# Fewer changes of TensorE tiling: row-tiled groups shifted by one tile across layer borders in a six-layer cross network

## The chip, the cores and the metric

The kernel runs on one core of a Trainium2 chip. The metric is the device time of one execution in microseconds (us), smaller is better. The times of before are three runs on the chip; the profile is one further execution taken by the hardware profiler. All times below are us from the start of the profiled span unless they are said to be run times. TensorE is called PE, its weight loads PEld, VectorE DVE, ScalarE ACT, GpSimd POOL, SyncE SP.

## The reference

```python
B, F, D, L = 4096, 26, 16, 6
Din = min(F * D, 1024)            # 416
# x0: [4096, 416], ws: [6, 416, 416], bs: [6, 416], all bf16
def reference(x0, ws, bs):
    x = x0
    for l in range(ws.shape[0]):
        x = x0 * (x @ ws[l] + bs[l]) + x
    return x
```

Six layers, each a 416 x 416 matrix product for 4096 rows, a bias, a product with x0 and a sum with the layer's input.

## The kernel before

**Layout.** For the first five layers the activations lie transposed: features on partitions, rows of the batch along the free dimension. The 416 features are three blocks of 128 (`XM`, index k or m) and a remainder of 32. The batch of 4096 is two halves s = 0, 1 of 2048 columns, each of four column groups g of 512. The remainder of the four groups of one half is stacked on the 128 partitions of `XR` (32 partitions for each g). `XM[0]`, `XR[0]` hold x0; `XM[1]`, `XM[2]` and `XR[1]`, `XR[2]` take turns as a layer's input and output.

**Three tilings of PE.** A 128-feature output block is made of two kinds of matmuls. The three main blocks contract 128 partitions: in the first layer as whole-array matmuls (`full` in `first_layer`, L240), in layers 1 to 4 *column-tiled* (`mm_full`, L205): four matmuls with 32 output columns each at positions (0, 0), (0, 32), (0, 64), (0, 96), which run side by side. The remainder contracts 32 partitions and is *row-tiled* (`mm_row`, L211; in the first layer `row`, L247): four matmuls at positions (0, 0), (32, 0), (64, 0), (96, 0), one for each column group. The product for the remainder's own 32 output features (`mm_rem`, L217 and L222) is column-tiled. A *tile* below is one output block m of one half s: four PSUM banks, as two pairs (`new_pts`, two calls of `two_banks`, which hands out the four pairs of banks in a fixed order).

**Order of work.** The order is written out by hand, each engine runs its instructions in program order. `first_layer(0)` and `first_layer(1)` do the first layer; `rem_first` the remainder of both halves at its end. In each of layers 1 to 4 the six tiles (0,0), (0,1), (0,2), (1,0), (1,1), (1,2), as (s, m), are worked in three couples ta, tb: `mm_full` of ta, then one row-tiled group that closes ta and opens tb (`mm_row` twice), then `mm_full` of tb. So each layer has three row-tiled groups. After the first couple come the remainders of both halves (`rem_pair`).

**Behind a tile.** `finish` calls `ew_main` for each pair of banks: ACT copies PSUM to a bf16 buffer `t` with the bias added (L169; six such buffers), which frees the banks; DVE multiplies by x0 (L179) and adds the layer's input (L180). The first layer folds the sum into the bias, so that DVE only multiplies (L177); `split_first` shares one pair between ACT (L186) and DVE (L187). `ew_rem` does the same for the remainder (L193, L198, L199).

**Last layer.** Here the roles are swapped: 128 rows of the batch are the output's partitions and 416 features its columns, so the result lies in row order. There are eight row tiles q (`quads`), each of four column groups g. Each needs 12 whole-array matmuls (`mm_q_full`, L357), and row-tiled ones for the remainder (L366) and the bias (L371) in `mm_q_rows`. Row tiles 0 to 5 go in couples with one row-tiled group each, 6 and 7 have one each: five groups. ACT casts (L383, single ones L396), DVE multiplies by `X0rows` (L384, L397) and adds `XLrows` (L385, L400), SP stores. `XLrows` is layer 4's output turned into row order: DMA transposes on SP for the main blocks (`xl_dmat`, L229), and for the remainder a DMA transpose into `scrR` (L299) and a copy by POOL (L300).

**Loads.** All go through SP's queue in the order of the code, but for the first layer's weights, the biases and the layer-0 rows of `WR`, which ACT issues at the start. `WR` holds the 32 remainder rows of the weights four times, once for each row position: for layer 0 one load and three copies by DVE (L113), for layers 1 to 5 four loads on SP. `WD` (POOL, L133) holds their block-diagonal form for the remainder's own product. `load_x0t` (L77) loads and transposes 512 columns of x0.

Of the kernel before, what the change touches and what calls it, by code (L numbers as in the profile page):

```python
# [10 lines left out]
ALU = mybir.AluOpType  # L11
BF16 = mybir.dt.bfloat16
# [4 lines left out]
def kernel(  # L17
# [7 lines left out]
    nc = tc.nc  # L25
    B, D = x0.shape
    L = ws.shape[0]
    P = 128
# [68 lines left out]
    load_x0t(0, 0)  # L97
    load_wm(nc.scalar, 0)
    nc.scalar.dma_start(bsb[0:L, :], bs[:, :])
    load_wr(nc.scalar, 0, 0, 1)  # L100
    nc.scalar.activation(dz[:, 1:2], dz[:, 0:1], ACT.Identity, bias=dz[:, 0:1], scale=1.0)

    nc.vector.transpose(out=bT[:], in_=bsb[0:R, :].rearrange("p (c r) -> p c r", r=R))
# [7 lines left out]
        nc.gpsimd.tensor_copy(bsb[32 * g:32 * g + 32, :], bsb[0:R, :])  # L111
    for g in range(1, NG):
        nc.vector.tensor_copy(WR[32 * g:32 * g + 32, 0, :], WR[0:32, 0, :])  # L113
    load_x0t(0, 1)
    load_xrem(nc.sync, 0, 0, 64)
    load_x0t(0, 2)
# [5 lines left out]
    load_x0t(1, 3)  # L122
    load_wm(nc.sync, 1)
    for g in range(NG):
        load_wr(nc.sync, g, 1, L)
    for l in range(2, L):
        load_wm(nc.sync, l)
    for q in range(8):
# [12 lines left out]

    def two_banks():
        n = turn[0]
        i = first_order[n] if n < len(first_order) else (2, 1, 3, 0)[(n - len(first_order)) % 4]
        turn[0] += 1
        return PS[:, 2 * i:2 * i + 2, :]

# [77 lines left out]
    def new_pts():  # L225
        return [two_banks() for h in range(2)]
# [4 lines left out]

    def first_layer(s):
        cur, nxt = XM[0], XM[1]

        def full(pt, m, h, gl, first, last):
            c0 = col0(s, 2 * h + gl)
            for k in range(NK):
                nc.tensor.matmul(pt[:, gl, :], lhsT=WM[:, 0, k, 128 * m:128 * m + 128], rhs=cur[:, k, c0:c0 + CW],  # L240
                                 start=(first and k == 0), stop=(last and k == NK - 1), skip_group_check=True)

        def row(pt, m, h, swapped, first):
            for gl in range(2):
# [14 lines left out]
        if s == 0:  # L259
            closing = [split_first(s, 0, 0, pa[0], nxt)]  # L260
            closing.append(split_first(s, 2, 0, pa[2], nxt))
            t1 = ew_copy(0, 1, pa[1])
            for close in closing:
                close()
            x0_rem(0, 64, 128, (nc.scalar.copy, nc.vector.tensor_copy))
            nc.vector.tensor_tensor(out=nxt[:, 1, 0:2 * CW], in0=t1, in1=XM[0][:, 1, 0:2 * CW], op=ALU.mult)
        else:
            split_first(s, 0, 0, pa[0], nxt)()
            for m in (2, 1):
                ew_main(0, s, m, 0, pa[m], cur, nxt)  # L270
        pb += [two_banks() for m in range(1, NK)]
        for m, gl in ((0, 0), (1, 0), (2, 0), (0, 1), (1, 1), (2, 1)) if s == 0 else ((0, 0), (1, 0), (0, 1), (1, 1), (2, 0), (2, 1)):
            full(pb[m], m, 1, gl, s == 0 or m > 0, s == 1 and m == 0)
            if s == 1 and (m, gl) == (0, 1):
                ew_main(0, s, 0, 1, pb[0], cur, nxt)
        if s == 0:
            row(pb[0], 0, 1, 0, False)
            row(pb[1], 1, 1, 0, False)
            row(pb[2], 2, 1, 1, False)
            split_first(s, 0, 1, pb[0], nxt)()  # L280
            x0_rem(1, 0, 128, (nc.vector.tensor_copy,))
            for m in range(1, NK):
                ew_main(0, s, m, 1, pb[m], cur, nxt)
        else:
            row(pb[1], 1, 1, 0, False)
            row(pb[2], 2, 1, 1, False)
            rem_first(pb)

    x0_rem(0, 0, 64, (nc.scalar.copy, nc.vector.tensor_copy))
    load_xrem(nc.scalar, 0, 64, 128)  # L290
# [9 lines left out]
                nc.gpsimd.tensor_copy(XLrows[:, 16 * s:16 * s + 16, NK * P:D].rearrange("p (g i) r -> p i g r", g=NG),  # L300
                                      scrR[s][:].rearrange("p i (g r) -> p i g r", g=NG))

    def rem_first(pb):
        pr2 = two_banks()
        for s in range(NS):
            mm_rem(0, s, pr2[:, s, :], XM[0], XR[0])
        for s in range(NS):
            ew_rem(0, s, pr2[:, s, :], XR[0], XR[1])
            ew_main(0, 1, 1 + s, 1, pb[1 + s], XM[0], XM[1])

    first_layer(0)
    fill_wd(1, L)
    first_layer(1)
    cur, curR = XM[1], XR[1]
    for l in range(1, LL):
        nxt, nxtR = XM[1 + (l % 2)], XR[1 + (l % 2)]
        feeds_last = (l == LL - 1)
        tiles = [(s, m) for s in range(NS) for m in range(NK)]
        pts = {}

        def finish(t):
            s, m = t
            for h in range(2):
                ew_main(l, s, m, h, pts[t][h], cur, nxt)
            if feeds_last:
                xl_dmat(s, m, nxt)

        for n in range(0, len(tiles), 2):
            ta, tb = tiles[n], tiles[n + 1]
            pts[ta] = new_pts()  # L330
            for g in range(NG):
                mm_full(l, ta[0], ta[1], g, pts[ta], cur, True, False)
            mm_row(l, ta[0], ta[1], pts[ta], curR, False, True)
            pts[tb] = new_pts()
            mm_row(l, tb[0], tb[1], pts[tb], curR, True, False)
            finish(ta)
            for g in range(NG):
                mm_full(l, tb[0], tb[1], g, pts[tb], cur, False, True)
            finish(tb)
            if n == 0:  # L340
                rem_pair(l, cur, curR, nxtR, feeds_last)
        cur, curR = nxt, nxtR

    l = LL
    quads = [(s, i) for s in range(NS) for i in range(4)]
    NQ = len(quads)
    KD = NK * P

    def q_cols(q, g):
        s, i = quads[q]  # L350
# [3 lines left out]
    def mm_q_full(q, py, gs, first):  # L354
        for g in gs:
            for k in range(NK):
                nc.tensor.matmul(py[g // 2][:, g % 2, 0:D], lhsT=cur[:, k, q_cols(q, g)], rhs=WM[:, l, k, :],  # L357
                                 start=(first and k == 0), stop=((not first) and k == NK - 1), skip_group_check=True)


# [1 line left out]
    def mm_q_rows(qs, pys, begun):  # L362
        for q, py in zip(qs, pys):
            s, i = quads[q]
            for g in range(NG):
                nc.tensor.matmul(py[g // 2][:, g % 2, 0:D], lhsT=curR[32 * g:32 * g + 32, CW * s + 128 * i:CW * s + 128 * i + 128],  # L366
                                 rhs=WR[32 * g:32 * g + 32, l, :], start=not (q == begun and g < 2), stop=False,
                                 tile_position=(32 * g, 0), skip_group_check=True)
        for q, py in zip(qs, pys):
            for g in range(NG):  # L370
                nc.tensor.matmul(py[g // 2][:, g % 2, 0:D], lhsT=pick[1][32 * g:32 * g + 32, :],  # L371
                                 rhs=bsb[32 * g:32 * g + 32, :], start=False, stop=(q == begun and g < 2), tile_position=(32 * g, 0),
                                 skip_group_check=True)

    o4 = [big.tile([P, NG, D], BF16, name=f"o4_{q}") for q in range(3)]

    def ew_pair(q, h, py):
        s, i = quads[q]
        b0 = 16 * s + 8 * h + i
        t = tpool.tile([P, 2 * CW], BF16, name="t")  # L380
        tv = t[:, 0:2 * D].rearrange("p (a d) -> p a d", a=2)
        o = o4[q][:, 2 * h:2 * h + 2, :] if q < 3 else opool.tile([P, 2, D], BF16, name="o")[:]
        nc.scalar.copy(tv, py[h][:, :, 0:D])  # L383
        nc.vector.tensor_tensor(out=tv, in0=tv, in1=X0rows[:, b0:b0 + 5:4, :], op=ALU.mult)  # L384
        nc.vector.tensor_tensor(out=o, in0=tv, in1=XLrows[:, b0:b0 + 5:4, :], op=ALU.add)  # L385
        if q >= 3:
            nc.sync.dma_start(out_v[:, b0:b0 + 5:4, :], o)
        elif h == 1:
            nc.sync.dma_start(out_v[:, b0 - 8:b0 + 5:4, :], o4[q][:])

    def ew_single(q, g, py):
        s, i = quads[q]
        b = 16 * s + 4 * g + i
        t = tpool.tile([P, 2 * CW], BF16, name="t")
        o = opool.tile([P, 2, D], BF16, name="o")
        nc.scalar.copy(t[:, 0:D], py[g // 2][:, g % 2, 0:D])  # L396
        nc.vector.tensor_tensor(out=t[:, 0:D], in0=t[:, 0:D], in1=X0rows[:, b, :], op=ALU.mult)  # L397

        def close():
            nc.vector.tensor_tensor(out=o[:, 0, :], in0=t[:, 0:D], in1=XLrows[:, b, :], op=ALU.add)  # L400
            nc.sync.dma_start(out_v[:, b, :], o[:, 0, :])

        return close

    for q in range(0, NQ - 2, 2):
        py = [new_pts()]
        mm_q_full(q, py[0], (0, 1), True)
        py.append(new_pts())
        mm_q_rows((q, q + 1), py, q)
        ew_pair(q, 0, py[0])  # L410
        mm_q_full(q, py[0], (2, 3), False)
        ew_pair(q, 1, py[0])
        for h in range(2):
            mm_q_full(q + 1, py[1], (2 * h, 2 * h + 1), False)
            ew_pair(q + 1, h, py[1])
    pending = []
    for q in range(NQ - 2, NQ):
        py = new_pts()
        mm_q_rows((q,), (py,), None)
        for g in range(NG):  # L420
            mm_q_full(q, py, (g,), False)
            pending.append(ew_single(q, g, py))
            keep = 0 if (q, g) in ((NQ - 2, NG - 1), (NQ - 1, 0), (NQ - 1, NG - 1)) else 1
            while len(pending) > keep:
                pending.pop(0)()


# [28 lines left out]
```

## Time and profile before

| What | Value |
|---|---|
| Run times, median (lowest to highest) of 3 | 130.79 us (130.72 to 131.23) |
| Profiled execution: its own time | 130.19 us |
| Profiled execution: span on the page | 128.1 us |
| PE busy, matmuls | 122.7 us (96%), 1677 |
| DVE busy | 105.2 us (82%) |
| ACT busy | 83.5 us (65%) |
| POOL busy | 8.6 us (7%) |
| Granted PE clock | 1.0 |
| L205 column-tiled matmuls | 1152, 379 ns each, 65.2 us busy together |
| L357 last layer, whole array | 96, 340 ns each, 17.9 us busy |
| L169 ACT copy of a pair of banks | 56, 1115 ns each |
| L179, L180 DVE, 1024 columns | 48 each, 695 and 699 ns |

Busy time of matmuls that run side by side counts once, so 1152 matmuls of 379 ns make 65.2 us. The end of a matmul in the profile is modelled, and pipelined matmuls overlap; the pace of PE is read from one start to the next. Idle time of an engine costs only where another waits for it.

### The profile page before, as it was taken

Reading aid. Unit: us, or ns where it says so; the run is one execution under the profiler, and the core shown is the slowest. Engines: PE = TensorE matmul, PEld = TensorE weight load, DVE = VectorE, ACT = ScalarE, POOL = GpSimd, SP = SyncE. Lnnn points to the kernel's source line nnn. Section 1 sums busy time; section 2 is a strip of 40 time slices with the busy share of each in tenths; the row PEclk is TensorE's granted clock in tenths of the full one; section 3 lists DMA queues with packets and bytes.
Section 4 is the critical chain, followed back from the end, with each engine's and each line's share of the span. In section 5 each row is a group of like instructions: output and inputs, shape, how many; then the busy total and the mean of one; then the engine's idle time right before and its main releaser. Section 6 shows DMA issues by size and latency. Waiting matters only on the chain. (4 is left out here: it accounts for less than half of the span.)

```text
span 128.1 us, 3929 instructions
## 1 busy us (share of the span) xinstructions
PE 122.7 (96%) x1677; PEld 54.7 (43%) x1677; DVE 105.2 (82%) x192; ACT 83.5 (65%) x94; POOL 8.6 (7%) x29
## 2 busy tenths in 40 slices
PE   6999999999999999999999999999999999999960
PEld 3344344444444444444444544444444445445420
DVE  3347959357979898989898989898989999999991
ACT  2117559489666849666849666749666777567860
POOL 4282000120000000000000000000000300000000
PEclk9999999999999999999999999999999999999999
DMA  3999999999990000000000000000398899986663
GB/s 91 259 157 192 207 187 263 229 329 332 336 314 24 5 0 8 0 0 5 0 5 0 5 0 5 0 0 5 69 140 177 167 122 246 192 283 216 210 225 103
DMA packets 42029, 16.36 MB, mean 128 GB/s; under 512 B 30838, under 2 KB 42012, under 8 KB 42012
## 3 DMA queue, kind: packets, MB, share of 16 engines
q1 hardware_dynamic: 40512, 15.70, 55.0%
q10 hardware_dynamic: 1500, 0.42, 1.6%
q8 instruction: 13, 0.21, 0.7%
q14 instruction: 4, 0.03, 0.1%
HBM read 6.15 MB, written 3.41 MB: 75 GB/s over the span
## 5 line engine op out<-in xcount | busy, mean ns | idle before, releaser
L169 ACT ACTIVATE t<-PS,bM 128x1024 bf16<-128x1024 f32 x56 | 58.1, 1115 | 21.2 <-PE PS L211 21.2
L205 PE MATMUL PS<-XM,WM 128*32 128x512 bf16 x1152 | 65.2, 379 | 0.0
L205 PEld LDWEIGHTS <-WM 128*32 128x32 bf16 x1152 | 29.8, 97 | 33.7 <-issue 5.1
L179 DVE TENSOR_TENSOR t<-t,XM 128x1024 bf16<-128x1024 bf16 x48 | 33.4, 695 | 4.1 <-ACT t L169 4.1
L180 DVE TENSOR_TENSOR XM<-t,XM 128x1024 bf16<-128x1024 bf16 x48 | 33.5, 699 | 3.1
L357 PE MATMUL PS<-WM,XM 128*128 128x416 bf16 x96 | 17.9, 340 | 0.0
L240 PE MATMUL PS<-XM,WM 128*128 128x512 bf16 x72 | 16.5, 383 | 0.1
L383 ACT CAST t<-PS 128x832 bf16<-128x832 f32 x12 | 10.2, 852 | 5.0 <-PE PS L357 2.5
L357 PEld LDWEIGHTS <-XM 128*128 128x128 bf16 x96 | 8.9, 98 | 8.7 <-issue 2.1
L240 PEld LDWEIGHTS <-WM 128*128 128x128 bf16 x72 | 6.9, 99 | 9.4 <-issue 2.1
L222 PE MATMUL PS<-XM,WM 128*32 128x512 bf16 x120 | 8.2, 379 | 0.0
L193 ACT ACTIVATE t<-PS,bR 128x512 bf16<-128x512 f32 x10 | 6.8, 694 | 1.9 <-POOL WD L133 1.9
L385 DVE TENSOR_TENSOR o<-t,XLrows 128x832 bf16<-128x832 bf16 x12 | 7.1, 592 | 0.5
L211 PE MATMUL PS<-XR,WR 32*128 32x512 bf16 x96 | 7.3, 379 | 0.0
L384 DVE TENSOR_TENSOR t<-t,X0rows 128x832 bf16<-128x832 bf16 x12 | 7.0, 586 | 0.0
L300 POOL COPY XLrows<-scrR 128x512 bf16<-128x512 bf16 x2 | 1.4, 698 | 72.7 <-DMA scrR<-XR 72.7
L177 DVE TENSOR_TENSOR XM<-t,XM 128x1024 bf16<-128x1024 bf16 x7 | 4.7, 690 | 1.5 <-ACT t L169 1.4
L150 PE MATMUL PS<-warm 128*128 128x512 bf16 (+2 forms) x13 | 4.6, 536 | 1.0 <-DVE warm L87 1.0
L186 ACT ACTIVATE t<-PS,bM 128x512 bf16<-128x512 f32 x4 | 2.6, 685 | 3.8 <-PE PS L247 3.8
L162 ACT COPY XR<-xrt 64x256 bf16<-64x256 bf16 x2 | 1.2, 621 | 5.7 <-DVE xrt L161 5.7
L161 DVE STREAM_TRANSPOSE xrt<-xrem 64x256 bf16<-64x256 bf16 (+1 forms) x5 | 2.2, 477 | 3.2 <-DMA xrem<-in_x_dram 3.2
L396 ACT CAST t<-PS 128x416 bf16<-128x416 f32 x8 | 4.0, 506 | 1.0 <-PE PS L357 0.8
(44 smaller groups left out, 54.4 us busy)
## 6 DMA issues: line engine op xcount, KB each, us to landing
X0rows<-in_x_dram SPq DMA_DIRECT2D x8, 416.0 KB, 7.5
WM<-in_ws_dram SPq DMA_DIRECT2D x5, 312.0 KB, 6.7
out_dram<-o SPq DMA_DIRECT2D x3, 416.0 KB, 3.2
out_dram<-o SPq DMA_DIRECT2D x6, 208.0 KB, 2.5
out_dram<-o SPq DMA_DIRECT2D x8, 104.0 KB, 1.7
WR<-in_ws_dram SPq DMA_DIRECT2D x4, 130.0 KB, 5.7
WM<-in_ws_dram ACTq DMA_DIRECT2D x1, 312.0 KB, 3.4
XM<-in_x_dram SPq DMA_TRANSPOSE x8, 4.8
```

Of the source, the lines that this page charges most:

```text
L169: nc.scalar.activation(t[:], pt.rearrange("p a b -> p (a b)"), ACT.Identity, bias=bM[:, m, l:l + 1], scale=1.0)
L179: nc.vector.tensor_tensor(out=t, in0=t, in1=x0c, op=ALU.mult)
L180: nc.vector.tensor_tensor(out=nxt[:, m, c0:c0 + 2 * CW], in0=t, in1=cur[:, m, c0:c0 + 2 * CW], op=ALU.add)
L193: nc.scalar.activation(tr[:, 0:CW], pr, ACT.Identity, bias=bR[:, l:l + 1], scale=1.0)
L205: nc.tensor.matmul(pts[g // 2][32 * q:32 * q + 32, g % 2, :], lhsT=WM[:, l, k, 128 * m + 32 * q:128 * m + 32 * q + 32], rhs=cur[:, k, c0:c ...
L211: nc.tensor.matmul(pts[g // 2][:, g % 2, :], lhsT=WR[32 * g:32 * g + 32, l, 128 * m:128 * m + 128], rhs=curR[32 * g:32 * g + 32, CW * s:CW ...
L222: nc.tensor.matmul(pr[32 * g:32 * g + 32, :], lhsT=WM[:, l, k, NK * P:D], rhs=cur[:, k, c0:c0 + CW], start=False, stop=(k == NK - 1), tile ...
L240: nc.tensor.matmul(pt[:, gl, :], lhsT=WM[:, 0, k, 128 * m:128 * m + 128], rhs=cur[:, k, c0:c0 + CW], start=(first and k == 0), stop=(last ...
L357: nc.tensor.matmul(py[g // 2][:, g % 2, 0:D], lhsT=cur[:, k, q_cols(q, g)], rhs=WM[:, l, k, :], start=(first and k == 0), stop=((not first ...
L383: nc.scalar.copy(tv, py[h][:, :, 0:D])
L384: nc.vector.tensor_tensor(out=tv, in0=tv, in1=X0rows[:, b0:b0 + 5:4, :], op=ALU.mult)
L385: nc.vector.tensor_tensor(out=o, in0=tv, in1=XLrows[:, b0:b0 + 5:4, :], op=ALU.add)
```

## The change

- Layers 1 to 4: the couples that share a row-tiled group move on by one tile. A group now closes the second tile of a couple and opens the first of the next; the last group of a layer opens tile (0,0) of the next layer. Each layer's first tile is thus already open, with four PSUM banks held, when the layer begins. The remainder pair (`rem_pair`) stands after the third tile instead of after the second.
- First layer: the half s = 1 uses column-tiled matmuls instead of whole-array ones. The remainder of s = 0 stands inside it (`rem_first(0)`), that of s = 1 after the first tile of layer 1 (`rem_first(1)`). Its last row-tiled group also opens layer 1.
- Last layer: the last group of layer 4 also holds the rows and biases of row tile 0; tiles 1 and 2, 3 and 4, 5 and 6 share a group, 7 has its own: four groups. Within a group the biases of a tile follow its rows. The last half of row tile 5 is handled in single column groups as 6 and 7 are, and the order of the DVE steps of the last three tiles is written out as a list.
- Loads: the layer-1 rows of `WR` come with those of layer 0 on ACT's queue, and ACT makes their three copies. The fixed order of bank pairs changes from (2, 1, 3, 0) to (2, 1, 0, 3).

```diff
-    load_wr(nc.scalar, 0, 0, 1)
+    load_wr(nc.scalar, 0, 0, 2)
...
         nc.vector.tensor_copy(WR[32 * g:32 * g + 32, 0, :], WR[0:32, 0, :])
+        nc.scalar.copy(WR[32 * g:32 * g + 32, 1, :], WR[0:32, 1, :])
...
-        load_wr(nc.sync, g, 1, L)
+        load_wr(nc.sync, g, 2, L)
...
-        i = first_order[n] if n < len(first_order) else (2, 1, 3, 0)[(n - len(first_order)) % 4]
+        i = first_order[n] if n < len(first_order) else (2, 1, 0, 3)[(n - len(first_order)) % 4]
...
-                nc.tensor.matmul(pt[:, gl, :], lhsT=WM[:, 0, k, 128 * m:128 * m + 128], rhs=cur[:, k, c0:c0 + CW],
-                                 start=(first and k == 0), stop=(last and k == NK - 1), skip_group_check=True)
+                for q0, q1 in ((0, P),) if s == 0 else [(32 * q, 32 * q + 32) for q in range(4)]:
+                    nc.tensor.matmul(pt[q0:q1, gl, :], lhsT=WM[:, 0, k, 128 * m + q0:128 * m + q1], rhs=cur[:, k, c0:c0 + CW],
+                                     start=(first and k == 0), stop=(last and k == NK - 1),
+                                     tile_position=(0, q0) if s == 1 else None, skip_group_check=True)
...
+        full(pb[0], 0, 1, 0, False, False)
+        rem_first(0)
+        pb += [two_banks() for m in range(1, NK)]
+        full(pb[1], 1, 1, 0, True, False)
+        full(pb[0], 0, 1, 1, False, True)
+        ew_main(0, s, 0, 1, pb[0], cur, nxt)
+        full(pb[1], 1, 1, 1, True, False)
+        for gl in range(2):
+            full(pb[2], 2, 1, gl, True, False)
+        row(pb[1], 1, 1, 0, False)
+        row(pb[2], 2, 1, 1, False)
+        pt = new_pts()
+        mm_row(1, 0, 0, pt, XR[1], True, False)
+        for m in range(1, NK):
+            ew_main(0, s, m, 1, pb[m], cur, nxt)
+        return pt
...
         for n in range(0, len(tiles), 2):
             ta, tb = tiles[n], tiles[n + 1]
-            pts[ta] = new_pts()
             for g in range(NG):
-                mm_full(l, ta[0], ta[1], g, pts[ta], cur, True, False)
-            mm_row(l, ta[0], ta[1], pts[ta], curR, False, True)
+                mm_full(l, ta[0], ta[1], g, pts[ta], cur, False, True)
+            close(ta)
+            if n == 0 and l == 1:
+                rem_first(1)
+            if n == 2:
+                rem_pair(l, cur, curR, nxtR, feeds_last)
             pts[tb] = new_pts()
-            mm_row(l, tb[0], tb[1], pts[tb], curR, True, False)
-            finish(ta)
             for g in range(NG):
-                mm_full(l, tb[0], tb[1], g, pts[tb], cur, False, True)
-            finish(tb)
-            if n == 0:
-                rem_pair(l, cur, curR, nxtR, feeds_last)
...
+                mm_full(l, tb[0], tb[1], g, pts[tb], cur, True, False)
+            mm_row(l, tb[0], tb[1], pts[tb], curR, False, True)
+            opened = new_pts()
+            if n + 2 < len(tiles):
+                tc_ = tiles[n + 2]
+                mm_row(l, tc_[0], tc_[1], opened, curR, True, False)
+                pts[tc_] = opened
+            elif not feeds_last:
+                mm_row(l + 1, 0, 0, opened, nxtR, True, False)
+            else:
+                mm_q_rows((0,), (opened,), None)
+            close(tb)
...
+    order = [(0, 0), (0, 1), (1, 0), (2, 0), (1, 1), (3, 0), (4, 0), (2, 1), (5, 0), (3, 1), (6, 0), (4, 1), (5, 1), (6, 1),
+             (7, 0), (8, 0), (7, 1), (9, 0), (8, 1), (10, 0), (9, 1), (10, 1)]
...
+    for h in range(2):
+        mm_q_full(0, opened, (2 * h, 2 * h + 1), False)
+        ew_pair(0, h, opened)
+    for q in range(1, NQ - 1, 2):
         py = [new_pts()]
         mm_q_full(q, py[0], (0, 1), True)
         py.append(new_pts())
         mm_q_rows((q, q + 1), py, q)
...
+    evict(NQ - 3, 0, 2, py[0])
+    for q in range(NQ - 3, NQ):
+        if q == NQ - 1:
+            py.append(new_pts())
+            mm_q_rows((q,), (py[2],), None)
+        for g in range(2 if q == NQ - 3 else 0, NG):
+            mm_q_full(q, py[q - NQ + 3], (g,), False)
+            evict(q, g, g + 1, py[q - NQ + 3])
```

`close` is `finish` under a new name. An entry (u, step) of `order` is the product (0) or the sum with its store (1) of unit u: unit 0 is the first half of row tile 5, units 1 and 2 its single column groups, 3 to 6 those of tile 6, 7 to 10 those of tile 7.

More of the change, by code (lines that the diff above doesn't have):

```diff
@@ L266, in first_layer @@
             nc.vector.tensor_tensor(out=nxt[:, 1, 0:2 * CW], in0=t1, in1=XM[0][:, 1, 0:2 * CW], op=ALU.mult)
[L267 to L276, printed above, removed]
+            pb += [two_banks() for m in range(1, NK)]
+            for m, gl in ((0, 0), (1, 0), (2, 0), (0, 1), (1, 1), (2, 1)):
+                full(pb[m], m, 1, gl, True, False)
             row(pb[0], 0, 1, 0, False)
@@ L283, in first_layer @@
                 ew_main(0, s, m, 1, pb[m], cur, nxt)
[L284 to L287, printed above, removed]
+            return None
+        split_first(s, 0, 0, pa[0], nxt)()
+        for m in (2, 1):
+            ew_main(0, s, m, 0, pa[m], cur, nxt)
+        full(pb[0], 0, 1, 0, False, False)
+        rem_first(0)
+        pb += [two_banks() for m in range(1, NK)]
+        full(pb[1], 1, 1, 0, True, False)
[11 more added lines that the diff above has]
+        return pt
     x0_rem(0, 0, 64, (nc.scalar.copy, nc.vector.tensor_copy))
@@ L301, in rem_pair, with rem_first @@
                                       scrR[s][:].rearrange("p i (g r) -> p i g r", g=NG))
[L303 to L309, printed above, removed]
+    def rem_first(s):
+        pr = two_banks()
+        mm_rem(0, s, pr[:, 0, :], XM[0], XR[0])
+        ew_rem(0, s, pr[:, 0, :], XR[0], XR[1])
@@ new lines, with q_cols, mm_q_full @@
+    xL, xLR = XM[1 + (LL - 1) % 2], XR[1 + (LL - 1) % 2]
+    quads = [(s, i) for s in range(NS) for i in range(4)]
+    NQ = len(quads)
+    def q_cols(q, g):
+        s, i = quads[q]
+        c = col0(s, g) + 128 * i
+        return slice(c, c + 128)
+    def mm_q_full(q, py, gs, first):
+        for g in gs:
+            for k in range(NK):
+                nc.tensor.matmul(py[g // 2][:, g % 2, 0:D], lhsT=xL[:, k, q_cols(q, g)], rhs=WM[:, LL, k, :],
+                                 start=(first and k == 0), stop=((not first) and k == NK - 1), skip_group_check=True)
@@ new lines, in mm_q_rows @@
+    def mm_q_rows(qs, pys, begun):
+        for q, py in zip(qs, pys):
+            s, i = quads[q]
+            for g in range(NG):
+                nc.tensor.matmul(py[g // 2][:, g % 2, 0:D], lhsT=xLR[32 * g:32 * g + 32, CW * s + 128 * i:CW * s + 128 * i + 128],
+                                 rhs=WR[32 * g:32 * g + 32, LL, :], start=not (q == begun and g < 2), stop=False,
+                                 tile_position=(32 * g, 0), skip_group_check=True)
+            for g in range(NG):
+                nc.tensor.matmul(py[g // 2][:, g % 2, 0:D], lhsT=pick[1][32 * g:32 * g + 32, :],
+                                 rhs=bsb[32 * g:32 * g + 32, :], start=False, stop=(q == begun and g < 2), tile_position=(32 * g, 0),
+                                 skip_group_check=True)
@@ L311, with close @@
     first_layer(0)
     fill_wd(1, L)
-    first_layer(1)
-    cur, curR = XM[1], XR[1]
+    opened = first_layer(1)
     for l in range(1, LL):
-        nxt, nxtR = XM[1 + (l % 2)], XR[1 + (l % 2)]
+        cur, curR = XM[1 + (l - 1) % 2], XR[1 + (l - 1) % 2]
+        nxt, nxtR = XM[1 + l % 2], XR[1 + l % 2]
         feeds_last = (l == LL - 1)
         tiles = [(s, m) for s in range(NS) for m in range(NK)]
-        pts = {}
-        def finish(t):
+        pts = {tiles[0]: opened}
+        def close(t):
@@ L336 @@
-            finish(ta)
             for g in range(NG):
-                mm_full(l, tb[0], tb[1], g, pts[tb], cur, False, True)
-            finish(tb)
-            if n == 0:
-                rem_pair(l, cur, curR, nxtR, feeds_last)
[L342 to L350, printed above, removed]
-        c = col0(s, g) + 128 * i
-        return slice(c, c + 128)
[L354 to L358, printed above, removed]
@@ L362, in mm_q_rows @@
[L362 to L373, printed above, removed]
@@ L375 @@
-    o4 = [big.tile([P, NG, D], BF16, name=f"o4_{q}") for q in range(3)]
+                mm_full(l, tb[0], tb[1], g, pts[tb], cur, True, False)
[9 more added lines that the diff above has]
+                mm_q_rows((0,), (opened,), None)
@@ L377, in ew_pair @@
+            close(tb)
+    o4 = [big.tile([P, NG, D], BF16, name=f"o4_{q}") for q in range(4)]
     def ew_pair(q, h, py):
@@ L381, in ew_pair @@
         tv = t[:, 0:2 * D].rearrange("p (a d) -> p a d", a=2)
-        o = o4[q][:, 2 * h:2 * h + 2, :] if q < 3 else opool.tile([P, 2, D], BF16, name="o")[:]
+        o = o4[q][:, 2 * h:2 * h + 2, :] if q < 4 else opool.tile([P, 2, D], BF16, name="o")[:]
         nc.scalar.copy(tv, py[h][:, :, 0:D])
@@ L385, in ew_pair @@
         nc.vector.tensor_tensor(out=o, in0=tv, in1=XLrows[:, b0:b0 + 5:4, :], op=ALU.add)
-        if q >= 3:
+        if q >= 4:
             nc.sync.dma_start(out_v[:, b0:b0 + 5:4, :], o)
@@ L389, in ew_pair, with ew_steps, product, total @@
             nc.sync.dma_start(out_v[:, b0 - 8:b0 + 5:4, :], o4[q][:])
-    def ew_single(q, g, py):
+    def ew_steps(q, g0, g1, py):
         s, i = quads[q]
-        b = 16 * s + 4 * g + i
+        b, n = 16 * s + 4 * g0 + i, g1 - g0
         t = tpool.tile([P, 2 * CW], BF16, name="t")
+        tv = t[:, 0:n * D].rearrange("p (a d) -> p a d", a=n)
         o = opool.tile([P, 2, D], BF16, name="o")
[L396 to L405, printed above, removed]
+        nc.scalar.copy(tv, py[g0 // 2][:, g0 % 2:g0 % 2 + n, 0:D])
+        def product():
+            nc.vector.tensor_tensor(out=tv, in0=tv, in1=X0rows[:, b:b + 4 * n - 3:4, :], op=ALU.mult)
+        def total():
+            nc.vector.tensor_tensor(out=o[:, 0:n, :], in0=tv, in1=XLrows[:, b:b + 4 * n - 3:4, :], op=ALU.add)
+            nc.sync.dma_start(out_v[:, b:b + 4 * n - 3:4, :], o[:, 0:n, :])
+        return product, total
+    order = [(0, 0), (0, 1), (1, 0), (2, 0), (1, 1), (3, 0), (4, 0), (2, 1), (5, 0), (3, 1), (6, 0), (4, 1), (5, 1), (6, 1),
+             (7, 0), (8, 0), (7, 1), (9, 0), (8, 1), (10, 0), (9, 1), (10, 1)]
+    units = []
+    def evict(q, g0, g1, py):
+        units.append(ew_steps(q, g0, g1, py))
+        while order and order[0][0] < len(units):
+            u, step = order.pop(0)
+            units[u][step]()
+    for h in range(2):
+        mm_q_full(0, opened, (2 * h, 2 * h + 1), False)
+        ew_pair(0, h, opened)
+    for q in range(1, NQ - 1, 2):
         py = [new_pts()]
@@ L409 @@
         mm_q_rows((q, q + 1), py, q)
[L410 to L425, printed above, removed]
+        if q < NQ - 3:
+            ew_pair(q, 0, py[0])
+            mm_q_full(q, py[0], (2, 3), False)
+            ew_pair(q, 1, py[0])
+            for h in range(2):
+                mm_q_full(q + 1, py[1], (2 * h, 2 * h + 1), False)
+                ew_pair(q + 1, h, py[1])
+    evict(NQ - 3, 0, 2, py[0])
[6 more added lines that the diff above has]
+            evict(q, g, g + 1, py[q - NQ + 3])
 _INS = ['x0', 'ws', 'bs']
```

## The prediction

> **What bounds the kernel now.** I read the page first, then TensorE's timeline, then VectorE's (DVE) through the border of the last layer, then ScalarE (ACT) and GpSimd (POOL) at two places. The page:
>
> ```profile
> PE 122.7 (96%) x1677; PEld 54.7 (43%) x1677; DVE 105.2 (82%) x192; ACT 83.5 (65%) x94; POOL 8.6 (7%) x29
> DVE  3347959357979898989898989898989999999991
> ```
>
> PE is dense from start to end, and the waits name no matmul that waits after the warm-up. But the DVE slices are full in the last quarter too. The PE timeline prices a change of tiling. Columns: start, length, engine, line, operation, count.
>
> ```profile
> 28.98 2.77 PE L205 MATMUL PS<-XM,WM 128*32 128x512 bf16 x48
> 31.58 0.39 PE L217 MATMUL PS<-XR,WD 128*32 128x512 bf16 x4
> ...
> 36.54 5.36 PE L205 MATMUL PS<-XM,WM 128*32 128x512 bf16 x96
> 41.84 0.61 PE L211 MATMUL PS<-XR,WR 32*128 32x512 bf16 x8
> 42.38 5.36 PE L205 MATMUL PS<-XM,WM 128*32 128x512 bf16 x96
> ```
>
> Read starts only. A step is four narrow matmuls side by side. From column to column (L205 to L217), 12 steps take 2.60: 0.2167 each. Into rows, 24 steps take 5.30, so 0.10 over 5.20. Out of rows, two steps take 0.54: 0.107 over. In the last layer:
>
> ```profile
> 100.09 2.77 PE L205 MATMUL PS<-XM,WM 128*32 128x512 bf16 x48
> 102.79 1.23 PE L357 MATMUL PS<-WM,XM 128*128 128x416 bf16 x6
> 103.95 0.56 PE L366 MATMUL PS<-WR,XR 32*128 32x416 bf16 x8
> 104.32 0.54 PE L371 MATMUL PS<-bsb,pick 32*128 32x416 bf16 x8
> 104.79 4.39 PE L357 MATMUL PS<-WM,XM 128*128 128x416 bf16 x24
> ...
> 115.07 3.34 PE L357 MATMUL PS<-WM,XM 128*128 128x416 bf16 x18
> ```
>
> Column to whole array, 100.09 to 102.79, is 2.70: 0.10 over 12 steps. From one full stretch to the next, 104.79 to 109.93 is 5.14 for 28 steps (24 full, 4 of rows), and 115.07 to 118.81 is 3.74 for 20. So a 416-wide step is 0.175 and a row group costs 0.24 beyond its steps. Now DVE and POOL across that border:
>
> ```profile
> 95.29 0.69 DVE L179 TENSOR_TENSOR t<-t,XM 128x1024 bf16<-128x1024 bf16 x1 [0.22 <-ACT t L169]
> ...
> 97.95 0.69 DVE L179 TENSOR_TENSOR t<-t,XM 128x1024 bf16<-128x1024 bf16 x1
> ...
> 99.35 1.10 DVE L179 TENSOR_TENSOR t<-t,XM 128x1024 bf16<-128x1024 bf16 x1
> 100.55 1.01 DVE L180 TENSOR_TENSOR XM<-t,XM 128x1024 bf16<-128x1024 bf16 x1
> ...
> 106.94 0.58 DVE L384 TENSOR_TENSOR t<-t,X0rows 128x832 bf16<-128x832 bf16 x1
> ```
> ```profile
> 99.11 0.79 POOL L300 COPY XLrows<-scrR 128x512 bf16<-128x512 bf16 x1 [72.22 <-DMA scrR<-XR]
> ```
>
> The wait at 95.29 is DVE's last over 0.1: from there it runs without a pause to its end at 125.39, and two of its operations stretch from 0.69 to over 1.0 just while POOL copies. PE's last step ends at 123.60 and the last cast at 124.31. The chain that ended last is all DVE from 116.61, with gaps of at most 0.10 until the final 0.25. So two engines reach the end within 0.1 us of each other, and a saving on PE counts only as far as DVE follows.
>
> **The change, part by part.** Let E be the first full matmul of the last layer: E = 102.79 before, E' after. Before, PE's last step ends at E+20.81, DVE's at E+22.60.
>
> *Row groups.* The matmuls are the same but for 36 full ones of the first layer that become 144 narrow ones. The order of the built program has 44 changes of tiling before and 41 after. In layers 1 to 4 the groups only shift: still three a layer. What goes is one group of the last layer (0.24) and the column-to-full change ahead of E (0.10). The last group now leaves to full tiling at 0.14 (103.95 to 104.79, less four steps) instead of 0.107. Sum: 0.31 saved. Because the first row tile of the last layer now stands ahead of it, E' is later by its two steps, 0.35, less 0.10, plus 0.03: +0.28; behind E', PE needs 20.81 - 0.35 - 0.24 = 20.22.
>
> The trace makes a change 0.10 to 0.11 us. The Trainium skill, TensorE: Matmul & The Clock Gate, Part 2 (DRAIN), speaks of about 128 cycles, an estimate of 0.053 us at the 2.4 GHz that it gives; the saving would then be some 0.16 instead of 0.31. The rows decide.
>
> *First layer, second half.* Column steps at 0.2167 in place of full ones at 0.216 (15.06 to 19.05 is 18 steps and one change): 36 x 0.001, nothing. The remainder of s=0 (0.87) is moved into it. Three steps after 19.60 stand at 20.25; it writes where ACT ends at 19.54 + 0.69 = 20.23, the 0.03 of delay that PE has there now too (20.28). It ends at 21.15. pb[1] then needs the copy of pa[2], which starts at 20.12 and takes 1.115: 21.235, some 0.05 to release: PE waits 0.13. Today pb[0]'s second column group waits at 20.71 to 21.00, 0.07 over a step, for the transposed load issued at 16.8 that lands 4.1 later; moved behind the remainder it no longer does. Net +0.06. Rows open layer 1 near 24.85: their XR (remainder: ACT to 22.9, DVE to 23.4) is there by 1.4, their banks (ACT to 23.9) by 0.9; without that cover each microsecond late is one on PE, since all of PE queues behind. WM of layer 1 landed at 18.39 + 4.4 = 22.8, needed at 25.2. The remainder of s=1 follows the first tile of layer 1; nobody needs it for 5 us.
>
> *Loads and copies at the start.* Three 32x416 copies join ACT. Nearest rows: DVE's same copy 0.29, ACT's 64x256 copy 0.62; so 0.9 to 1.9 us, between WR's landing at 5.9 and ACT's next work at 8.81: hidden; uncovered, the first rows (9.90) would move by what sticks out. WR's first load grows by 26 KB and shares the rings with the first transposed load, which lands at 5.71 exactly where real matmuls start. At the slice's 259 GB/s that is 0 to 0.10; nothing shows how it falls, I take the middle, +0.05. WR for layers 2 up keeps its place on SP.
>
> *Layers 1 to 4.* The remainder pair moves behind the third tile. On SP its two transposes of XR (1.26 each) pass behind one more transpose of XM (2.9); POOL's copies follow, due before the last layer's first sum, over 4 us later: free. Openings wait for the remainder's DVE end; in layer 4 that is 5 us early. They need a bank pair whose tile closed 2.9 before; ACT frees it within 1.5: covered by 1.4.
>
> So E' = E + 0.28 + 0.06 + 0.05 = E + 0.39, and PE ends at E + 0.39 + 20.22 = E + 20.61, 0.20 earlier.
>
> *DVE to the end.* Behind E' - 0.705 (the last row group: 0.217 + 0.35 + 0.14) lie 5.30 of two tiles and 0.54 of rows: tile (1,0) now closes with the group that starts at E' - 6.545. A tile closed by rows reaches DVE 1.58 later (93.71 to 95.29): E' - 4.965. DVE is idle there: the second and third tile (from E' - 12.5, 5.4) and the remainder pair (1.8) are done at E' - 5.3. From there, tiles (1,0), (1,1), (1,2) take 8.99 (97.95 to 106.94, POOL's two copies within, as they will be: transposes of XR land at E' - 1.6 and - 0.3). The last layer starts on DVE at S = E' + 4.03; before it was E + 4.15. Then pairs: 13.68 for 12 (106.94 to 120.62), 1.14 each; 11 remain, 12.54. Singles: 0.285 apart (121.19 to 122.33 is four); 20 instead of 16, 5.70, and 0.09 for the last one's full 0.37. End: E' + 4.03 + 18.33 = E + 22.75. PE would allow E + 22.40. DVE is late next: **+0.15 us**. SP's last outputs go 0.44 apart, 17 as before: no change behind.
>
> The profiled execution is 130.19 (span 128.1, 2.1 around it); 130.34 after. The median of the runs is 0.6 above it: 130.79 + 0.15 = 130.94, say 130.9.
>
> **Rivals.**
> 1. *PE's end sets the time.* If POOL's copies cost DVE less (they cost 8.99 - 3 x 2.72 = 0.83), S falls toward E' + 3.2 and PE's E + 22.40 rules: -0.20, 130.6. It decides at S = E' + 3.68. Without the start's +0.11, -0.31. For: only those 0.83 make DVE the later one. Against: the copies stay as long, and DVE is as busy beside them.
> 2. *PE waits for PSUM in each row group.* An opening takes four banks of a tile closed one tile earlier. If DVE's lag keeps the six t buffers full, ACT stalls; beyond the 1.4 of cover, each 0.1 late is 0.1 in each of 12 groups: 1.2 us, 132.0. For: DVE works 18.2 of each layer's 19.23. Against: DVE catches up in every layer (0.2 to 0.6 idle ahead of a tile), and today's openings have the same spacing.
> 3. *Narrow weight loads bind in the first layer.* A 128x32 load shows 97 ns, as a 128x128 one. One after another, four are 0.39 against 0.217: 36 x 0.17 = 6.2 us, 137.0. The Trainium skill, TensorEngine Tiling (Array Packing), Gotcha 2, says that column tiling excludes the fast weight load. Against: 1152 such matmuls already run at 0.2167 a step.
> 4. *The groups don't go away.* Then nothing is saved and the end is DVE's all the same, within 0.3 of the forecast (about 131.0); the program's order excludes it.
>
> **How the numbers follow.** Forecast 0.45 (130.7 to 131.1); rival 1 0.27 (130.3 to 130.7); rival 2 0.12; rival 3 0.02; rival 4 none; 0.14 for what I don't see, more of it faster than slower. About 0.5% (0.65 us) is what a measurement of this kernel tells from no change. Forecast and rival 1 lie inside it: 0.71 with a little of the rest. Slower by more: rivals 2 and 3 and some unseen, 0.17. Faster by more: 0.12, as three changes of tiling hold 0.34 at most. The range takes the forecast, rival 1 and the lower part of rival 2: 130.3 to 131.5.
>
> **What would show it.** Right: 41 changes; about 0.24 less in the last layer's PE; XR rows ahead of the first full stretch; a PE wait near 21.2; DVE without idle from the close of (1,0) to its end, and the last cast over 0.2 us ahead of the last product. Wrong: DVE waits for casts at the end (rival 1), PE gaps at row groups (rival 2), steps over 0.22 between 15 and 25 us (rival 3), or real matmuls starting later than 5.8.

## The result and the profile after

The changed kernel takes 131.41 us (median of 19 runs, 130.84 to 131.91) against 130.64 us for the kernel before, run beside it on the same chip: ratio 1.0053, interval 1.0038 to 1.0069. That is 0.77 us slower, just beyond what the prediction called no change, and inside its range (130.3 to 131.5) but 0.5 us above its value. The profiled execution took 131.37 us (span 129.6); that of the kernel before was 0.45 us below its median, so the two profiles lie 1.2 us apart where the medians lie 0.77.

The page of the changed kernel, first and second part:

```profile
PE 122.6 (95%) x1784; PEld 55.6 (43%) x1785; DVE 105.5 (81%) x194; ACT 85.3 (66%) x98; POOL 8.9 (7%) x29
DVE  3357849648497989898989898989898999999991
```

PE's busy time is the same to 0.1 us while the span grew by 1.5. So PE waits somewhere, and its timeline shows where (columns as before the change; in brackets, idle time and what ended it):

```profile
15.13 4.07 PE L244 MATMUL PS<-XM,WM 128*32 128x512 bf16 x72
19.66 0.61 PE L252 MATMUL PS<-XR,WR 32*128 32x512 bf16 x6 [0.46 <-DVE XR L163]
...
21.27 0.83 PE L244 MATMUL PS<-XM,WM 128*32 128x512 bf16 x12 [0.90 <-DMA XM<-in_x_dram]
...
103.94 0.40 PE L212 MATMUL PS<-XR,WR 32*128 32x512 bf16 x4
...
104.62 3.34 PE L335 MATMUL PS<-WM,XM 128*128 128x416 bf16 x18
...
122.72 2.28 PE L335 MATMUL PS<-WM,XM 128*128 128x416 bf16 x12
```

Two waits, 1.36 us together, in the first layer's half s=1: 0.46 for XR (x0's remainder: its load came late, DVE prepared it late) and 0.90 for a transposed load of x0. In steps, with the prediction's own numbers:

| Stretch | before | after | difference | forecast |
|---|---|---|---|---|
| start to the row group after s=1's first half | 19.05 | 19.66 | +0.61, of it 0.46 wait | +0.05 |
| from there to the last layer's first full matmul | 83.74 | 84.96 | +1.22, of it 0.90 wait | +0.34 |
| from there to the end of PE's last step | 20.81 | 20.20 | -0.61 | -0.59 |
| from the last layer's first full matmul to DVE's end | 22.60 | 22.17 | -0.43 | -0.24 |

The first, second and last line add up to +1.40. Without the two waits it would be +0.04. The DVE side at the border of the last layer:

```profile
99.68 0.69 DVE L180 TENSOR_TENSOR t<-t,XM 128x1024 bf16<-128x1024 bf16 x1 [0.22 <-ACT t L170]
...
103.68 1.10 DVE L180 TENSOR_TENSOR t<-t,XM 128x1024 bf16<-128x1024 bf16 x1
...
106.25 0.99 DVE L181 TENSOR_TENSOR XM<-t,XM 128x1024 bf16<-128x1024 bf16 x1
...
108.48 0.58 DVE L404 TENSOR_TENSOR t<-t,X0rows 128x832 bf16<-128x832 bf16 x1
```

It waits last at 99.68, which is 4.94 ahead of the first full matmul (forecast 4.965), stretches twice beside POOL's copies as before, and begins the last layer 3.86 behind it (forecast 4.03).

What held up the load? The DMA view of the changed kernel from 18.25 to 20.25 us, 40 slices of 0.05 us, then the packets by queue:

```profile
GB/s 261 312 282 297 276 302 609 261 276 261 195 0 0 0 0 0 0 0 0 0 0 0 0 0 5 5 10 5 10 10 5 10 10 10 5 15 5 15 5 10
...
q1 hardware_dynamic: 614, 0.16, 131.8%
q8 instruction: 1, 0.02, 2.9%
```

From 18.8 to past 20 us the DMA engines move next to nothing (0 to 15 GB/s). Just before stands one packet of 16 KB (0.02 MB) on queue 8, a fetch of instructions; it starts at 18.57, is the 609 in its slice, and the transposed load's packets behind it take up to 1.55 us instead of 0.02. The kernel before makes its first such fetch at 21.69. Its view from 21.5 to 23.5 us, when plain loads of weights are in flight:

```profile
GB/s 416 316 333 628 300 250 250 300 150 216 200 116 183 250 150 150 184 200 150 167 200 216 100 250 233 200 133 216 166 167 233 283 216 283 233 233 250 150 216 166
```

The fetch is the 628, and nothing stops.

The wait for XR is another matter. The remainder's load had landed when DVE began to transpose it, 0.3 us before that fetch:

```profile
18.27 0.71 DVE L162 STREAM_TRANSPOSE xrt<-xrem 128x512 bf16<-128x512 bf16 x1 [1.85 <-DMA xrem<-in_x_dram]
```

In experiments 1 and 3 too it landed ahead of the fetch (18.47 against 19.43, 18.07 against 18.32), and experiment 4 below has such a wait with no fetch near. So the 0.46 is not the fetch's work. Whether the narrow matmuls have a part in it stays open: the three traces with narrow ones in the first six blocks of s=1 wait 0.41 to 0.64, the five with whole ones and no early fetch between nothing and 0.53.

So from the first result there were three theories for the 0.9: narrow matmuls as such slow the loads, the new loads do, or chance; and after the first four runs a fourth, the instruction fetch (theory F).

### The profile page after: what moved, and what is told of

Read it like the earlier page. It is cut to its first block, busy times and chain, and to the rows that moved or that the text cites. A ratio compares the mean times of both kernels' runs of the same rounds, so it can differ in the third digit from the quotient of the medians.

```text
span 129.6 us, 4149 instructions
## 1 busy us (share of the span) xinstructions
PE 122.6 (95%) x1784; PEld 55.6 (43%) x1785; DVE 105.5 (81%) x194; ACT 85.3 (66%) x98; POOL 8.9 (7%) x29
## 5 line engine op out<-in xcount | busy, mean ns | idle before, releaser
L206 PEld LDWEIGHTS <-WM 128*32 128x32 bf16 x1152 | 29.7, 97 | 33.8 <-issue 5.1
L244 PE MATMUL PS<-XM,WM 128*32 128x512 bf16 (+1 forms) x179 | 16.8, 382 | 1.0 <-DMA XM<-in_x_dram 0.9
L244 PEld LDWEIGHTS <-WM 128*32 128x32 bf16 (+1 forms) x180 | 7.6, 98 | 9.7 <-issue 2.8
L403 ACT CAST t<-PS 128x832 bf16<-128x832 f32 x10 | 8.4, 854 | 3.3 <-PE PS L335 2.1
L418 ACT CAST t<-PS 128x416 bf16<-128x416 f32 (+1 forms) x11 | 5.9, 538 | 1.6 <-PE PS L348 0.7
L405 DVE TENSOR_TENSOR o<-t,XLrows 128x832 bf16<-128x832 bf16 x10 | 5.9, 592 | 0.5
L404 DVE TENSOR_TENSOR t<-t,X0rows 128x832 bf16<-128x832 bf16 x10 | 5.8, 584 | 0.0
L223 PEld LDWEIGHTS <-WM 128*32 128x32 bf16 x120 | 3.3, 97 | 3.2
```

The costliest lines, as they stand in the source:

```text
L206: nc.tensor.matmul(pts[g // 2][32 * q:32 * q + 32, g % 2, :], lhsT=WM[:, l, k, 128 * m + 32 * q:128 * m + 32 * q + 32], rhs=cur[:, k, c0:c ...
L223: nc.tensor.matmul(pr[32 * g:32 * g + 32, :], lhsT=WM[:, l, k, NK * P:D], rhs=cur[:, k, c0:c0 + CW], start=False, stop=(k == NK - 1), tile ...
L244: nc.tensor.matmul(pt[q0:q1, gl, :], lhsT=WM[:, 0, k, 128 * m + q0:128 * m + q1], rhs=cur[:, k, c0:c0 + CW], start=(first and k == 0), sto ...
L418: nc.scalar.copy(tv, py[g0 // 2][:, g0 % 2:g0 % 2 + n, 0:D])
```

## Experiments

**1. Column tiling alone.** The kernel before, with this part of the change:

```diff
+                for q0, q1 in ((0, P),) if s == 0 else [(32 * q, 32 * q + 32) for q in range(4)]:
+                    nc.tensor.matmul(pt[q0:q1, gl, :], lhsT=WM[:, 0, k, 128 * m + q0:128 * m + q1], ...
```

> The kernel before, with one part of the change alone: the half s=1 of the first layer column-tiled (36 whole-array matmuls become 144 narrow ones), order, loads and row groups as before. Theory 1 (while narrow matmuls run, the transposed loads of x0 that are still arriving land later, and PE waits for them): the last two transposed loads land 6 to 7 us after their issue instead of 4 to 5, PE waits 0.6 to 1.4 us between 19 and 22 us, time 0.5 to 1.2 us above before (ratio 1.004 to 1.009). Theory 2 (the larger first load of WR and ACT's three copies delay the loads): no change, ratio 1.000, loads land as before. Theory 3 (the loads scatter by chance, whatever PE does): ratio 1.000 within 0.15%.

Measured: 131.64 us, ratio 1.0085 (1.0061 to 1.0109). In its profile the load issued at 14.1 landed 7.4 later, and PE waited:

```profile
19.86 0.61 PE L249 MATMUL PS<-XR,WR 32*128 32x512 bf16 x6 [0.64 <-DVE XR L162]
...
21.50 4.07 PE L241 MATMUL PS<-XM,WM 128*32 128x512 bf16 x72 [0.93 <-DMA XM<-in_x_dram]
```

The column tiling of s=1 by itself costs what the whole change costs, by the median more, as the savings are absent. Chance and the new loads are out as causes.

**2. Only the second half column-tiled.** The changed kernel with

```diff
-                for q0, q1 in ((0, P),) if s == 0 else [(32 * q, 32 * q + 32) for q in range(4)]:
+                for q0, q1 in ((0, P),) if s == 0 or h == 0 else [(32 * q, 32 * q + 32) for q in range(4)]:
...
-                                     tile_position=(0, q0) if s == 1 else None, skip_group_check=True)
+                                     tile_position=(0, q0) if s == 1 and h == 1 else None, skip_group_check=True)
```

> The changed kernel, but the first six blocks of s=1 (h=0, until about 19 us) whole-array again; only its second half (h=1), which runs when the transposed loads have nearly all landed, stays column-tiled. Changes of tiling: as in the changed kernel. Theory 1: the loads land as before (4 to 5 us), no PE wait over 0.2 near 20 us, and what is left is the prediction's sum: 0.2 us faster to 0.15 slower than before (ratio 0.998 to 1.001). Theory 2 and theory 3: as the changed kernel, ratio about 1.005.

Measured: 130.18 us, ratio 0.9977 (0.9957 to 0.9997).

```profile
19.46 0.61 PE L252 MATMUL PS<-XR,WR 32*128 32x512 bf16 x6 [0.15 <-DVE XR L163]
...
20.10 0.83 PE L244 MATMUL PS<-XM,WM 128*32 128x512 bf16 x12
...
103.52 3.34 PE L335 MATMUL PS<-WM,XM 128*128 128x416 bf16 x18
```

The wait for XR shrinks to 0.15 and the one for the load is gone, though the load issued at 14.2 landed 5.7 later and not 4 to 5. From the row group to the last layer's first full matmul are 84.06 us, the changed kernel's 84.96 less its wait (0.90 idle, 0.97 read from start to start).

**3. and 4. The loads alone.** The changed kernel with the old loads (the diff below), and the kernel before with the new ones (the same lines the other way round):

```diff
-    load_wr(nc.scalar, 0, 0, 2)
+    load_wr(nc.scalar, 0, 0, 1)
...
-        nc.scalar.copy(WR[32 * g:32 * g + 32, 1, :], WR[0:32, 1, :])
...
-        load_wr(nc.sync, g, 2, L)
+        load_wr(nc.sync, g, 1, L)
```

> The changed kernel, with WR's layer-1 rows loaded as before (four loads on SP for layers 1 to 5, no copies on ACT). Theory 1: the waits near 20 us stay, ratio about 1.005; the rows that open layer 1 (26.4 us) find WR landed (about 26) or wait up to 0.5. Theory 2: the waits go, ratio 0.998 to 1.001. Theory 3: ratio about 1.005 with a scatter as before.

> The kernel before, with the loads of the change alone (WR of layers 0 and 1 by ACT's queue, three copies on ACT, four smaller loads on SP). Theory 1: at most the 0.05 to 0.14 at the start, ratio 1.000 to 1.001. Theory 2: 0.5 to 1.2 us slower, ratio 1.004 to 1.009. Theory 3: ratio 1.000.

Measured: 131.48 us, 1.0068 (1.0045 to 1.0091) with the old loads; 130.49 us, 1.0000 (0.9984 to 1.0016) with the new ones in the kernel before. The loads neither cost nor heal anything that these runs can tell, which is 0.2 us. With the old ones the rows that open layer 1 wait 0.21 for WR, which is what the new ones are there for. The run of experiment 4 waits for XR too, with whole-array matmuls throughout and its fetch at 21.94:

```profile
19.73 0.61 PE L248 MATMUL PS<-XR,WR 32*128 32x512 bf16 x6 [0.53 <-DVE XR L163]
```

That wait comes and goes without the column tiling; the profiled execution of the kernel before had none.

**5. and 6. More instructions, no narrow matmuls.** In the traces of 1 to 4 a hold-up of 1.5 us stood wherever a 16 KB fetch met transposed loads of x0 (19.43 in 1, 18.32 in 3), and none over 0.8 us where it came later (22.09 in 2, 21.94 in 4). Four narrow matmuls are eight instructions with their weight loads where a whole one is two, so PE needs its next block earlier. The test: the kernel before with its warm-up cut into more pieces, and the first layer untouched.

```diff
-    pe_filler(9, CW)
+    pe_filler(5, CW)      # experiment 6: 2
+    pe_filler(27, 64)     # experiment 6: 54
```

> The kernel before with no matmul of the first layer changed; only the warm-up differs: four of its nine 512-column matmuls give way to 27 of 64 columns, so that PE has 46 more instructions ahead of the first layer. Theory F (a 16 KB fetch of PE's instructions, due when PE has come some 200 to 260 instructions far, holds up the transposed loads in flight for 1.5 us): the fetch moves from about 21.7 to 17 to 19 us, a load of x0 lands 1.2 us or more later than before, PE waits 0.6 to 1.2 us for it, ratio 1.004 to 1.010. Theory R (narrow matmuls read their moving operand four times and take bandwidth from the loads): no change, ratio 0.999 to 1.001.

> As the last one, with seven of the nine 512-column matmuls replaced by 54 of 64 columns: 94 more PE instructions. Theory F: the fetch comes at 12 to 15 us, the transposed load in flight there (for columns needed at 15.1 or 16.4 us) lands over 1 us late, and PE waits for it there instead of near 20; ratio 1.003 to 1.010. Theory R: ratio 0.999 to 1.001, unless the warm-up itself gets longer, which the start of the first real matmul shows.

Measured: 131.33 us, 1.0066 (1.0041 to 1.0090), and 131.63 us, 1.0075 (1.0047 to 1.0103). The real matmuls start at 5.46 and 5.62, no later than before (5.71). The fetch moves to 16.52 and 13.07, and the hold-up with it. Experiment 5, DMA from 16.5 to 18.5 us, and PE:

```profile
GB/s 396 51 26 51 92 113 128 123 113 159 174 159 179 200 189 113 87 82 97 67 67 46 36 51 41 46 10 10 10 10 5 15 5 15 5 15 113 271 287 302
```
```profile
19.78 0.61 PE L248 MATMUL PS<-XR,WR 32*128 32x512 bf16 x6 [0.69 <-DVE XR L163]
```

Experiment 6, from 13 to 15.5 us (slices of 0.0625), and PE:

```profile
GB/s 474 220 200 194 205 205 209 209 201 205 229 135 0 0 0 0 0 0 0 0 0 8 4 8 8 12 8 8 8 12 8 8 12 8 12 131 279 275 255 291
```
```profile
12.82 2.10 PE L241 MATMUL PS<-XM,WM 128*128 128x512 bf16 x9 [0.24 <-DMA XM<-in_x_dram]
16.57 0.60 PE L248 MATMUL PS<-XR,WR 32*128 32x512 bf16 x4 [1.65 <-DVE XR L163]
```

In 6 next to nothing moves from 13.75 to 15.2 us (at most 12 GB/s), and PE waits 1.65 us there instead of near 20, in an execution 0.7 us above the median. In 5 the pause is shorter (17.8 to 18.3, after a second at a third of the rate) and PE's wait is for XR, 0.69, rather than for a load of x0 itself, which landed 6.2 after its issue against 5.1: the size came as expected, the place one step aside. This trace by itself doesn't separate theory F from the wait of 0.53 that experiment 4 has without a fetch there. The times do (1.0066 against 1.0000), and so does experiment 6. Theory F holds; that narrow matmuls as such slow the loads is not needed, and here there were none.

**7. All of the first layer whole-array.** The changed kernel with `full` as before, so two changes of tiling more.

> The changed kernel with all of the first layer whole-array again; the remainder inside the second half stays, so there are 43 changes of tiling instead of 41. Theory F: the fetch comes after 21 us, no long hold-up. The price of a change of tiling read from the trace before (0.10 to 0.11): from the last rows of the first half to the last layer's first full matmul 0.2 us more than the changed kernel without its load wait; ratio 0.998 to 1.001. Theory R: the same.

Measured: 130.84 us, 1.0025 (1.0008 to 1.0042): slower than expected. From the row group to the last layer's first full matmul (19.18 to 103.70) are 84.52 us; 0.33 of that is a wait for a load (0.41 from start to start), so 84.1 to 84.2, about 0.1 above experiment 2 for two more changes (expected 0.2). The fetch comes at 21.97, 0.4 after the last transposed load landed (17.1 + 4.5). The price of two changes doesn't account for the whole distance to experiment 2 (0.6 us by the ratios). The wait follows a pause of the transposed loads at 19.3 to 20.0 us, with no fetch ahead of it; whether a fetch meets the last load in some of the runs was not seen. This stays open.

**8. XLrows' remainder by ACT.** Experiment 2 with POOL's two copies moved to ACT, the first between tiles (1,1) and (1,2):

```diff
...
-                nc.gpsimd.tensor_copy(XLrows[...], scrR[s][...])
...
+            if n == 4 and feeds_last:
+                xl_rem(0)      # nc.scalar.copy of the same
...
+            if q == 1:
+                xl_rem(1)
```

> The kernel with only the second half of s=1 column-tiled, and POOL's two copies into XLrows made by ACT, where ACT is idle (between tiles (1,1) and (1,2), and after row tile 1). Theory D (DVE sets the end of the changed kernel because its operations stretch beside POOL's copies): no DVE operation above 0.75 us there, DVE begins the last layer 0.5 to 0.8 us earlier relative to PE, and the end moves by the small rest by which DVE trails PE, 0.06 to 0.17 us; ratio 0.996 to 0.998. If PE sets the end, the same start of DVE but no gain: 0.9977 as without it. If POOL isn't the cause, the stretched operations stay.

Measured: 130.09 us, 0.9968 (0.9951 to 0.9985), the fastest of all. DVE and ACT:

```profile
102.77 0.69 DVE L181 TENSOR_TENSOR XM<-t,XM 128x1024 bf16<-128x1024 bf16 x1
104.05 0.69 DVE L180 TENSOR_TENSOR t<-t,XM 128x1024 bf16<-128x1024 bf16 x1 [0.59 <-ACT t L170]
```
```profile
102.39 0.62 ACT L316 COPY XLrows<-scrR 128x512 bf16<-128x512 bf16 x1 [1.35 <-DMA scrR<-XR]
102.91 2.11 ACT L170 ACTIVATE t<-PS,bM 128x1024 bf16<-128x1024 f32 x2
```

No operation is stretched any more, so POOL's copies were the cause. But the expected early start of DVE did not come: it is done with the tiles so far and waits 0.59 for tile (1,2). ACT's copy stands ahead of that tile and is 0.17 of it (ACT takes the tile 0.08 us ahead of the last layer's first full matmul, against 0.25 in experiment 2). The other 0.42 would stand without the copy, as PE closes the tile no earlier. DVE begins the last layer 3.73 behind the first full matmul, against 3.76 in experiment 2, and ends 1.07 after the last cast instead of 1.14. The intervals of 2 and 8 overlap; that 8 is faster than 2 is not shown, that it is faster than both the kernel before and the changed one is.

## Why the prediction came out as it did

*Row groups: right.* The last layer's PE stretch is 20.20 where 20.22 was forecast, and its first full matmul comes 0.32 later, measured from the row group and without waits (84.06 less 83.74), where 0.28 + 0.06 was forecast. Three changes of tiling fewer are worth what the rows said, 0.3 us. (The 44 and 41 of the prediction count the stretches of one tiling in the timelines; the changes between them are 43 and 40.)

*DVE late next: right in kind, over-sized.* DVE runs without a pause from tile (1,0) to the end, 1.24 us behind the last cast, where experiment 8 ends 1.07 behind it. Its stretch to the last layer was 8.80 instead of 8.99, and its start 3.86 instead of 4.03: the two slowed operations cost less than in the one execution that the price came from. The reason was in part another as well: in experiment 8 nothing was slowed, and DVE still started at 3.73, as it had to wait for the last tile. From experiments 2 and 8 its start can't come before about 3.56, an estimate (ACT hands the tile over at 0.89, 104.41 less 103.52, and DVE's four operations take 2.67, 104.05 to 106.72). The prediction had no term for that. So the net of everything but the narrow first half is not the +0.15 that was forecast but about -0.3 us (experiment 2, 0.9977).

*First layer, second half: this step failed.* Its "36 x 0.001, nothing" is true of PE's pace: the 72 narrow matmuls of the first half take 4.07, the 18 whole ones took 4.06. It priced the narrow matmuls by PE alone and not by what four times the instructions pull in: the next 16 KB block came at 18.57 instead of 21.69, in the middle of the transposed loads, for the last of which the same paragraph had shown PE to wait 0.07 us already. The load issued at 14.1 landed 7.1 later, not 5.1. By the ratios that is 0.9 to 1.1 us, shown by experiments 1, 5 and 6 in one direction and 2 in the other. The wait for XR, which the fetch doesn't explain, may be a part of it in the changed kernel and in experiment 1. The forecast value missed by the difference of this and the over-sized DVE term; the range held by luck, because the two have opposite signs, not because the cost was seen.

*Start: nothing.* The 0.05 for the larger load is too small to be told in experiment 4 (1.0000, 0.2 us either way).

*Rivals.* The price of rival 1 (PE's end alone) is close to what is left when the fetch is out of the way: experiments 2 and 8 gained 0.35 to 0.39 us where -0.20 to -0.31 stood. Its mechanism isn't shown: in both the chain that ended last still runs over DVE, and without POOL's copies DVE's start fell to 3.73, not toward 3.2 or below the 3.68 at which PE was to decide. No PE gap appears at a row group of layers 1 to 4 (rival 2). Narrow loads did not bind (rival 3). The wrong-sign mechanism was one that no rival named, and the sign "PE steps over 0.22 between 15 and 25 us" looked for it at the wrong place: steps kept their pace, and the waits stood between them.

## What to carry to other kernels

Count instructions, not only time: a tiling that turns one matmul into four brings the next instruction block forward, and where that fetch met DMA transposes for which an engine waits with no slack, it cost about a microsecond here. Use narrow tiles behind the last transposed load (experiment 2). More instructions ahead moved the fetch to a worse place in experiments 5 and 6; that moving it can also avoid the transposes was not tried. Look for the instruction queue in the DMA view when a load is late without reason. A saving on the busiest engine is worth its size only if the engine that closes the chain follows, so work out both ends.

## What the runs showed of the hardware

A fetch of PE's instructions stops DMA transposes, not plain loads. Thirteen or fourteen 16 KB fetches lie in each run, about one for 256 matmuls and weight loads. In the ten traces 27 of them meet the 256-byte packets of a transpose (a 28th meets only its last four). Each time some of these packets stay pending for 0.5 to 1.6 us, in 20 of the 27 for 1.2 or more, where 0.02 is the rule; at most 48 GB/s move meanwhile, and the pause ends 0.7 to 1.1 us after the fetch does. An 8 KB instruction packet on queue 14 does the same once in each trace, between 109 and 112 us, for 0.8 to 1.0 us. Packets of a transpose are pending without a fetch as well, for up to 0.94 us (experiment 1, at 16.8), but never over 1.0. Beside 832-byte packets of weights or x0 the traffic goes on: none in flight with a 16 KB fetch took over 0.55 us. A plain load in flight together with transposes is held up with them: in experiment 6 the remainder's, issued at 8.8, landed 6.5 later instead of 4.0.

The kernel before has it too, in the transposes ahead of its last layer, where nobody waits (103 to 105.5 us, 0.0625 us a slice; the fetch at 103.19 is the 430):

```profile
GB/s 234 258 430 213 238 254 94 25 16 0 0 0 0 0 0 0 0 4 12 4 8 8 8 8 12 12 4 12 12 8 61 295 242 12 57 287 291 291 287 287
```

The Trainium skill, Runtime: NRT & Kernel Launch, Instruction fetch mechanics, says that an engine's instructions come in blocks of 16 KiB, 256 instructions, by a DMA queue of their own, at a cost that is mostly hidden. The traces agree on the block and the count (16 KB packets, 14 of them for the 3569 matmuls and weight loads on the changed kernel's page), and hidden it is beside plain loads; beside DMA transposes packets waited up to 1.6 us. Why a transpose stops, and for longer than the fetch itself, no run here shows.
